# A new static order for the recorded part of a fused attention and MLP kernel: maxima apart from multiplies on Pool, transposes by TensorE, divisions on VectorE

## The chip, the cores and the metric

The kernel runs on one core of a Trainium2 chip. The metric is the device time of one execution in microseconds (us). TensorE does the matmuls, VectorE (DVE in the profile), ScalarE (ACT) and Pool (GpSimd) the element-wise work, and SyncE (SP) and Pool issue the DMAs. Runs are called fast or slow by their granted TensorE clock and time; only fast runs are compared here. Each kernel has one trace, of one of its runs: what a trace shows need not be the same in the others.

## The reference, cut to what matters

Favor attention (a random-feature softmax) over 8 batches of 8 heads with 576 tokens of 64 numbers, then a two-layer MLP with a GELU-like gate over the 4,608 tokens.

```python
def phi(x):                                   # q and k (times 64 ** -0.25), each token and head
    h = x @ omega.T - sum(x * x) / 2          # 64 -> 128 features
    return exp(h - max(h)) / sqrt(m)
kv  = einsum('bhsm,bhsd->bhmd', k_p, v);  z = sum(k_p, axis=2)
num = einsum('bhsm,bhmd->bhsd', q_p, kv)
den = einsum('bhsm,bhm->bhs', q_p, z) + 1e-06
x   = (num / den), heads side by side         # 4608 x 512
h   = x @ w_in                                # 512 -> 2048
out = (h / (1 + exp(-1.702 * h))) @ w_out     # 2048 -> 512
```

Sums over tokens make each batch of attention a unit; the MLP works on blocks of 512 tokens. A "pair" is two heads of one batch: batch 0 has pairs 0 to 3, batch 1 pairs 4 to 7, and so on. MLP block 0 needs batch 0; block 1 needs the last 64 tokens of batch 0 and most of batch 1, so all of pairs 4 to 7.

## The kernel before

The helpers that matter here are these. Both kernels have them at the same lines, so L390 or L509 in a profile is the same helper in both.

```python
def load_win(j):                               # L96, a quarter of w_in, issued by Pool
    nc.gpsimd.dma_start(win[j][:], ...)
def cast_k(b, c0, c1):                         # L160: DRAM to DRAM, float32 to bf16, issued by Pool
    nc.gpsimd.dma_start(sk[...], bass.AP(k.tensor, ...))
def cast_q(b, c0, c1): ...                     # L174: the same for q
def load_tr(b, n, c0, c1):                     # L179: DMA transpose of what the casts wrote
    nc.sync.dma_start_transpose(tiles[b][n][...], tiles[b]["s" + n][...])

def halves_max(p):                             # L390: first half of a row maximum, on VectorE
    ke = st[p, "ke"]
    nc.vector.tensor_tensor(out=half[:], in0=ke[:, :, 0:64], in1=ke[:, :, 64:128], op=ALU.max)
def maxima(p): ...                             # L395 reduce_max of half
def inverse(p): ...                            # L399 reciprocal
def scale_v(p, pool):                          # L406 and L412: v times the inverse maximum
    eng = nc.gpsimd if pool else nc.vector
    eng.tensor_tensor(out=vp[:, :, 0:64], in0=v, in1=emax, op=ALU.mult)
    eng.tensor_copy(out=vp[:, :, 64], in_=emax[:])

def nd_div(p, i, on_act=False): ...            # L461 ScalarE or L465 VectorE: num / den
def xt_pe(p, home): ...                        # L499: attention output of a pair transposed by TensorE
def xt_cp(p, on_act, c0=0, c1=S): ...          # and copied from PSUM into xt
def xt_dma(p):                                 # L509, L513: the same by two DMA transposes
    nc.sync.dma_start_transpose(dst[:, 0:512]..., xb[:, 0:4, :]...)
    nc.sync.dma_start_transpose(dst[:, 512:S], xb[64:128, 4, :])

def mm1(i, f, c0=0, c1=CM):                    # L545: w_in group f of block i; reads xt[0..3]
    for c in range(c0, c1):
        nc.tensor.matmul(ph, lhsT=win[f // 4][...], rhs=xt[c][:, i * TB : (i + 1) * TB], ...)
def gelu_th(i, f): ...                         # L561 tanh on ScalarE
def gelu_mul(i, f): ...                        # L569 multiply on VectorE, writes gTs[i][:, f]
def mm2_mms(i, r, part, home): ...             # L585: w_out, four groups f of token chunk r
```

All engines run a static order. For the first 80 us it is a recorded list of some 500 calls; after it a regular loop takes over. The old list around the start of block 1 reads:

```python
        load_v(2, 0, 2, nc.gpsimd)
        ...
        load_q(2, 2, 3)
        cast_q(3, 2, 3)
        cast_k(3, 0, 1)
        ...
        cast_q(3, 0, 1)
        kv_pe(7)
        xt_dma(4)
        ...
        xt_dma(5)
        ...
        cast_k(3, 1, 2)
        ...
        cast_q(3, 1, 2)
        mm2_store(0, 0)
        xt_dma(6)
        ...
        xt_dma(7)
        ...
        cast_k(3, 2, 3)
        load_bt(3, 0, 2)
        ...
        homes[1, 3] = "b0"
        mm1(1, 3)                              # the first w_in group of block 1
```

The softmax here doesn't subtract the row's maximum and nothing guards it: scores larger than these inputs give would overflow.

Of the kernel before, what the change touches and what calls it, by code (L numbers as in the profile page):

```python
# [21 lines left out]
def kernel(  # L22
# [16 lines left out]
    nc = tc.nc  # L39

    B, H, S, D = q.shape
# [658 lines left out]
    with tc.manual_schedule(engines={ET.DVE, ET.Activation}):  # L700
        load_k(0, 2, 3)
# [3 lines left out]
        make_identity(nc, ident[:])  # L705
        warm_mm(7, 512, "qp")
        tk_pe(0, "xx")
        q0_cast(True)
        load_q(0, 1, 2)
        om_cast(False)  # L710
        om_pe("b0")
        q0_cast(False)
        warm_mm(3, 128, "qp")
        tq_pe(0, "b1")
        tq_cp(0, True)
        om_cp(False)
        tk_cp(0, False)
        pk_pe(0)
        e_km(0)
        load_v(0, 0, 1, nc.gpsimd)  # L720
        tk_pe(1, "b0")
        tk_cp(1, False)
        tk_pe(2, "b1")
        load_q(0, 2, 3)
        tk_cp(2, False)
        pf_pe(0)
        e_k5(0)
        pq_pe(0)
        pk_pe(1)
        e_km(1)  # L730
        halves_max(0)
        load_q(0, 3, 4)
        pf_pe(1)
        tq_pe(1, "b1")
        pf_pe(2)
        maxima(0)
        e_k5(1)
        warm_mm(2, 512, "b0")
        pk_pe(2)
        load_k(0, 3, 4)  # L740
        load_v(0, 1, 2, nc.gpsimd)
        inverse(0)
        pr_pe(0)
        tq_cp(1, False)
        warm_mm(3, 128, "b0")
        pr_pe(1)
        load_k(1, 2, 3)
        e_qm(0)
        halves_max(1)
        maxima(1)  # L750
        tq_pe(2, "b0")
        tq_cp(2, False)
        warm_mm(3, 128, "b1")
        tk_pe(3, "b1")
        inverse(1)
        load_v(0, 2, 4, nc.gpsimd)
        load_k(1, 0, 1)
        tk_cp(3, False)
        e_k5(2)
        pq_pe(1)  # L760
        e_qr(0)
        e_km(2)
        halves_max(2)
        e_qm(1)
        tq_pe(3, "b0")
        load_q(1, 1, 2)
        load_k(1, 1, 2)
        tq_cp(3, False)
        load_win(0)
        pr_pe(2)  # L770
        pf_pe(3)
        scale_v(0, True)
        kv_pe(0)
        maxima(2)
        kv_cp(0)
        pk_pe(3)
        scale_v(1, True)
        warm_mm(1, 512, "b1")
        nd_pe(0, 1, "b1")
        e_qr(1)  # L780
        e_k5(3)
        inverse(2)
        scale_v(2, True)
        nd_pe(0, 0, "b0")
        nd_inv(0, 0)
        pr_pe(3)
        kv_pe(1)
        nd_inv(0, 1)
        nd_div(0, 0, False)
        e_km(3)  # L790
        halves_max(3)
        maxima(3)
        pq_pe(2)
        tk_pe(6, "kp")
        tk_cp(6, False)
        kv_cp(1)
        nd_pe(1, 0, "b0")
        nd_div(0, 1, True)
        inverse(3)
        xt_dma(0)  # L800
        nd_pe(1, 1, "b1")
        load_win(2)
        nd_inv(1, 1)
        e_qm(2)
        kv_pe(2)
        kv_cp(2)
        e_qr(3)
        scale_v(3, True)
        e_qr(2)
        nd_inv(1, 0)  # L810
        load_win(1)
        nd_div(1, 1, True)
        pq_pe(3)
        load_win(3)
        nd_div(1, 0, False)
        e_qm(3)
        tk_pe(4, "kp")
        tk_cp(4, False)
        tq_pe(5, "xx")
        load_q(1, 2, 3)  # L820
        tq_cp(5, False)
        nd_pe(2, 1, "b0")
        nd_pe(2, 0, "b1")
        pk_pe(4)
        nd_inv(2, 0)
        nd_inv(2, 1)
        nd_div(2, 0, False)
        nd_div(2, 1, False)
        load_k(2, 0, 1)
        load_q(1, 3, 4)  # L830
        kv_pe(3)
        kv_cp(3)
        xt_pe(1, "qp")
        xt_cp(1, False, 0, S2)
        xt_cp(1, False, S2, S)
        e_km(4)
        nd_pe(3, 0, "b1")
        nd_inv(3, 0)
        nd_pe(3, 1, "b0")
        homes[0, 0] = "xx"  # L840
        mm1(0, 0, 0, 1)
        nd_inv(3, 1)
        nd_div(3, 0, False)
        homes[0, 1] = "xx+"
        mm1(0, 1, 0, 1)
        mm1(0, 1, 1, 2)
        xt_pe(2, "kp")
        xt_cp(2, False, S2, S)
        tk_pe(5, "b1")
        xt_cp(2, False, 0, S2)  # L850
        nd_div(3, 1, True)
        xt_pe(3, "qp")
        xt_cp(3, False, 0, S2)
        mm1(0, 0, 1, 2)
        mm1(0, 0, 2, 3)
        homes[0, 3] = "b0"
        mm1(0, 3, 0, 1)
        xt_cp(3, False, S2, S)
        mm1(0, 1, 2, 3)
        mm1(0, 0, 3, 4)  # L860
        tk_cp(5, False)
        homes[0, 11] = "qp"
        mm1(0, 11)
        homes[0, 10] = "qp+"
        mm1(0, 10)
        gelu_th(0, 11)
        gelu_mul(0, 11)
        gelu_th(0, 0)
        gelu_th(0, 10)
        gelu_mul(0, 10)  # L870
        homes[0, 8] = "kp"
        mm1(0, 8)
        gelu_th(0, 8)
        mm1(0, 1, 3, 4)
        gelu_mul(0, 0)
        homes[0, 7] = "kp+"
        mm1(0, 7)
        gelu_th(0, 1)
        gelu_th(0, 7)
        homes[0, 4] = "b1"  # L880
        mm1(0, 4)
        gelu_mul(0, 8)
        homes[0, 9] = "qp+"
        mm1(0, 9)
        gelu_mul(0, 1)
        mm1(0, 3, 1, 2)
        gelu_th(0, 4)
        mm1(0, 3, 2, 3)
        gelu_th(0, 9)
        load_k(1, 3, 4)  # L890
        gelu_mul(0, 7)
        gelu_mul(0, 4)
        gelu_mul(0, 9)
        pk_pe(5)
        pf_pe(4)
        pf_pe(5)
        e_k5(4)
        homes[0, 12] = "b1"
        mm1(0, 12)
        halves_max(4)  # L900
        maxima(4)
        inverse(4)
        load_q(1, 0, 1)
        e_km(5)
        load_v(1, 2, 4, nc.gpsimd)
        homes[0, 6] = "qp+"
        mm1(0, 6)
        e_k5(5)
        homes[0, 13] = "kp+"
        mm1(0, 13)  # L910
        halves_max(5)
        load_v(1, 0, 2, nc.gpsimd)
        gelu_th(0, 12)
        gelu_mul(0, 12)
        load_wout(0)
        gelu_th(0, 6)
        gelu_th(0, 13)
        load_wout(1)
        gelu_mul(0, 13)
        homes[0, 14] = "qp"  # L920
        mm1(0, 14)
        gelu_th(0, 14)
        mm1(0, 3, 3, 4)
        gelu_th(0, 3)
        gelu_mul(0, 14)
        tk_pe(7, "xx")
        tk_cp(7, True)
        homes[0, 15] = "kp"
        mm1(0, 15)
        gelu_mul(0, 3)  # L930
        homes[0, 2] = "kp+"
        mm1(0, 2, 0, 1)
        load_wout(2)
        tq_pe(4, "b1")
        mm1(0, 2, 1, 2)
        mm1(0, 2, 2, 3)
        tq_cp(4, False)
        mm1(0, 2, 3, 4)
        gelu_th(0, 15)
        gelu_mul(0, 15)  # L940
        load_q(2, 0, 1)
        gelu_th(0, 2)
        tk_pe(8, "b0")
        tk_cp(8, True)
        homes[0, 5] = "b1"
        mm1(0, 5)
        gelu_th(0, 5)
        gelu_mul(0, 6)
        scale_v(4, True)
        pr_pe(5)  # L950
        pf_pe(7)
        pr_pe(4)
        pq_pe(4)
        e_qm(4)
        kv_pe(4)
        gelu_mul(0, 2)
        load_wout(3)
        pk_pe(6)
        pf_pe(6)
        e_k5(6)  # L960
        mm2_mms(0, 1, 0, "b0")
        e_k5(7)
        load_k(2, 2, 3)
        gelu_mul(0, 5)
        maxima(5)
        inverse(5)
        mm2_mms(0, 0, 0, "b1")
        kv_cp(4)
        e_km(6)
        tq_pe(6, "qp")  # L970
        tq_cp(6, False)
        halves_max(6)
        load_v(2, 2, 4, nc.gpsimd)
        mm2_mms(0, 1, 1, "b0")
        load_q(2, 1, 2)
        e_qr(5)
        e_qr(4)
        pq_pe(5)
        e_qm(5)
        maxima(6)  # L980
        inverse(6)
        pk_pe(7)
        scale_v(6, True)
        mm2_mms(0, 0, 1, "b1")
        mm2_mms(0, 0, 2, "b1")
        load_k(2, 1, 2)
        load_q(2, 3, 4)
        pr_pe(6)
        e_km(7)
        pq_pe(6)  # L990
        scale_v(5, False)
        halves_max(7)
        maxima(7)
        pf_pe(8)
        e_qm(6)
        kv_pe(5)
        e_k5(8)
        kv_cp(5)
        mm2_mms(0, 1, 2, "b0")
        nd2_pe(4, "qp")  # L1000
        mm2_mms(0, 1, 3, "b0")
        e_qr(6)
        nd2_pe(5, "xx")
        nd2_inv(4)
        nd2_div(4)
        load_v(2, 0, 2, nc.gpsimd)
        inverse(7)
        nd2_inv(5)
        tq_pe(8, "kp")
        nd2_div(5)  # L1010
        mm2_mms(0, 0, 3, "b1")
        tq_pe(7, "qp")
        scale_v(7, True)
        load_k(2, 3, 4)
        tq_cp(8, False)
        mm2_out(0, 1, True)
        tk_pe(10, "b0")
        kv_pe(6)
        pk_pe(8)
        tq_cp(7, False)  # L1020
        pq_pe(7)
        mm2_out(0, 0, True)
        tk_cp(10, False)
        load_q(2, 2, 3)
        cast_q(3, 2, 3)
        cast_k(3, 0, 1)
        mm2_mms(0, 2, 0, "b0")
        e_km(8)
        tk_pe(9, "b1")
        kv_cp(6)  # L1030
        nd2_pe(6, "xx")
        halves_max(8)
        tk_cp(9, False)
        mm2_mms(0, 2, 1, "b0")
        tq_pe(9, "b1")
        pk_pe(9)
        nd2_inv(6)
        nd2_div(6)
        e_qm(7)
        tq_cp(9, False)  # L1040
        pq_pe(8)
        pr_pe(7)
        e_km(9)
        cast_q(3, 0, 1)
        kv_pe(7)
        xt_dma(4)
        pf_pe(9)
# [276 lines left out]
```

## Time and profile before

| | before |
|---|---|
| time, median of three runs | 320.04 us (319.91 to 320.26) |
| profiled span | 317.0 us, clock 1.0 |
| TensorE busy | 309.5 us, 98% |
| VectorE, ScalarE, Pool busy | 197.4, 189.0, 86.1 us |
| longest maximum by halves | 2.14 us (median 459 ns) |

The stretches below show busy time of each engine with its instructions, granted clock, DMA share (over 1 where queues overlap in the records), and GB/s.

```profile
18.00:24.00 6.00, 5.41 (x86) 4.05 (x86) 5.08 (x20) 4.37 (x14) 5.72 (x9) 1.00 1.22 163
...
54.00:60.00 6.00, 6.00 (x79) 3.48 (x78) 5.00 (x12) 4.71 (x12) 0.18 (x1) 1.00 1.31 219
60.00:66.00 6.00, 6.00 (x72) 3.34 (x69) 3.56 (x7) 5.59 (x10) 3.36 (x6) 1.00 1.21 182
66.00:72.00 6.00, 6.00 (x98) 3.59 (x98) 5.62 (x14) 5.78 (x13) 1.32 (x2) 1.00 1.16 292
```

The timeline of TensorE (start, duration, engine, line, operation and tiles, count, and in brackets idle time with what ended it) at the start of block 1 and at the seam with the loop has no bracket at all:

```profile
61.86 0.38 PE L284 MATMUL pq<-qT,omT 64*128 64x512 bf16 x2
62.18 1.04 PE L545 MATMUL ph<-xt,win 128*128 128x512 bf16 x4
63.06 0.47 PE L441 MATMUL nd<-kvs,qe 128*128 128x65 bf16 x10
...
80.45 1.03 PE L585 MATMUL po<-wout,gT 128*128 128x512 bf16 x4
```

The change aims at the maxima. The view of one tile gives minimum, median and maximum in ns, and Pool's timeline shows what ran at the time of the long one (11.82 to 13.96 us):

```profile
L390 DVE TENSOR_TENSOR half<-ke x32: 397/459/2143, 8.0 to 231.0; 128x576 bf16<-128x576 bf16 x32
```

```profile
11.24 1.17 POOL L406 TENSOR_TENSOR vp<-vst,emax 128x576 bf16<-128x576 f32 x1
...
12.50 1.14 POOL L406 TENSOR_TENSOR vp<-vst,emax 128x576 bf16<-128x576 f32 x1
```

### The profile page before, as it was taken

Reading aid. Unit: us, or ns where it says so; the run is one execution under the profiler, and the core shown is the slowest. Engines: PE = TensorE matmul, PEld = TensorE weight load, DVE = VectorE, ACT = ScalarE, POOL = GpSimd, SP = SyncE. Lnnn points to the kernel's source line nnn. Section 1 sums busy time; section 2 is a strip of 40 time slices with the busy share of each in tenths; the row PEclk is TensorE's granted clock in tenths of the full one; section 3 lists DMA queues with packets and bytes.
Section 4 is the critical chain, followed back from the end, with each engine's and each line's share of the span. In section 5 each row is a group of like instructions: output and inputs, shape, how many; then the busy total and the mean of one; then the engine's idle time right before and its main releaser. Section 6 shows DMA issues by size and latency. Waiting matters only on the chain.

```text
span 317.0 us, 6672 instructions
## 1 busy us (share of the span) xinstructions
PE 309.5 (98%) x2647; PEld 165.2 (52%) x2647; DVE 197.4 (62%) x379; ACT 189.0 (60%) x364; POOL 86.1 (27%) x154
## 2 busy tenths in 40 slices
PE   8889999999999999999999999999999999999995
PEld 4565556555455555555555455555555444444444
DVE  3987878699566666666666666677774343343400
ACT  4887866897566666666666666666653434444311
POOL 8795446413511161116110430001010100001100
PEclk9999999999999999999999999999999999999999
DMA  8999999998798679775979395911122100001121
GB/s 189 249 170 221 272 244 223 204 261 143 98 297 170 133 199 209 141 126 156 227 102 190 74 274 135 193 54 35 54 35 64 57 35 33 34 33 35 47 85 67
DMA packets 61742, 44.13 MB, mean 139 GB/s; under 512 B 46161, under 2 KB 54736, under 8 KB 61392
## 3 DMA queue, kind: packets, MB, share of 16 engines
q0 software_dynamic: 13552, 24.55, 37.1%
q1 hardware_dynamic: 47888, 19.10, 29.0%
q8 instruction: 20, 0.33, 0.4%
q10 hardware_dynamic: 272, 0.07, 0.1%
q14 instruction: 10, 0.08, 0.1%
HBM read 37.42 MB, written 15.66 MB: 167 GB/s over the span
## 4 chain that ended last, share of the span: by engine, by line
PE 93%; DVE 3%; DMA 2%; ACT 0%; issue 0%; ACTq 0%; DVEq 0%
PE ph L545 40%; PE po L585 38%; PE xx L226 3%; PE nd L441 3%; PE pk L269 3%; PE pq L284 2%; DMA xt<-xb 2%; PE po L622 1%; PE warm_ps L681 1%; DVE half L390 1%; PE tk L198 1%; PE tq L211 1%; DVE maxE L395 1%; DVE qT L191 0%; DVE kT L191 0%; PE xx L284 0%
## 5 line engine op out<-in xcount | busy, mean ns | idle before, releaser
L545 PE MATMUL ph<-xt,win 128*128 128x512 bf16 x576 | 145.2, 379 | 0.2 <-DMA xt<-xb 0.2
L561 ACT ACTIVATE th<-ph 128x512 bf16<-128x512 f32 x144 | 86.2, 608 | 92.8 <-PE ph L545 92.7
L585 PE MATMUL po<-wout,gT 128*128 128x512 bf16 x560 | 141.5, 379 | 0.0
L569 DVE SCALAR_TENSOR_TENSOR gT<-th,ph 128x512 bf16<-128x512 bf16 x144 | 97.0, 684 | 63.3 <-ACT th L561 63.1
L545 PEld LDWEIGHTS <-win 128*128 128x128 bf16 x576 | 62.8, 114 | 55.1 <-DMA xt<-xb 0.7
L585 PEld LDWEIGHTS <-gT 128*128 128x128 bf16 x560 | 52.4, 98 | 59.0 <-issue 0.3
L608 POOL DMA_DIRECT2D out_dram<-osb x44 | 23.6, 539 | 178.2 <-ACT osb L598 175.2
L360 ACT ACTIVATE ke<-pk 128x1024 bf16<-128x1024 f32 x32 | 32.9, 1028 | 2.1 <-PE pk L269 2.0
L372 ACT ACTIVATE qe<-pq 128x1024 bf16<-128x1024 f32 x32 | 33.1, 1035 | 1.6 <-PE pq L284 1.5
L390 DVE TENSOR_TENSOR half<-ke 128x576 bf16<-128x576 bf16 x32 | 16.8, 524 | 26.8 <-ACT ke L369 23.6
L598 ACT ACTIVATE osb<-po 128x512 f32<-128x512 f32 x35 | 21.0, 599 | 18.7 <-PE po L585 18.6
L395 DVE TENSOR_REDUCE maxE<-half 128x9 f32<-128x576 bf16 x32 | 24.1, 753 | 0.9
L484 DVE TENSOR_TENSOR xb<-nd,rden 128x640 bf16<-128x640 f32 x28 | 23.1, 824 | 0.9
L406 POOL TENSOR_TENSOR vp<-vst,emax 128x576 bf16<-128x576 f32 x12 | 14.2, 1179 | 27.8 <-DVE emax L399 16.3
L441 PEld LDWEIGHTS <-qe 128*128 128x128 bf16 x320 | 14.0, 98 | 8.1 <-issue 1.5
L441 PE MATMUL nd<-kvs,qe 128*128 128x65 bf16 x320 | 15.6, 194 | 1.3 <-ACT xb L461 0.6
L226 PE MATMUL xx<-vp,ke 64*128 64x65 bf16 x576 | 15.8, 191 | 0.5 <-POOL vp L412 0.4
L406 DVE TENSOR_TENSOR vp<-vst,emax 128x576 bf16<-128x576 f32 x20 | 15.1, 757 | 0.8
L226 PEld LDWEIGHTS <-ke 64*128 64x128 bf16 x576 | 13.1, 95 | 2.1 <-issue 1.3
L269 PEld LDWEIGHTS <-qk 64*128 64x128 bf16 x180 | 7.6, 119 | 9.5 <-issue 6.9
L160 POOL DMA_DIRECT2D sk<-in_k_dram x20 | 10.9, 544 | 0.0
L174 POOL DMA_DIRECT2D sq<-in_q_dram x20 | 10.4, 518 | 0.0
(60 smaller groups left out, 183.9 us busy)
## 6 DMA issues: line engine op xcount, KB each, us to landing
vst<-in_v_dram SPq DMA_DIRECT2D x5, 1152.0 KB, 8.9
out_dram<-osb POOLq DMA_DIRECT2D x12, 256.0 KB, 2.4
sk<-in_k_dram POOLq DMA_DIRECT2D x19, 160.0 KB, 7.5
vst<-in_v_dram POOLq DMA_DIRECT2D x5, 576.0 KB, 8.9
sq<-in_q_dram POOLq DMA_DIRECT2D x20, 144.0 KB, 7.7
win<-in_moe_w_in_dram POOLq DMA_DIRECT2D x4, 512.0 KB, 7.5
wout<-in_moe_w_out_dram POOLq DMA_DIRECT2D x4, 512.0 KB, 10.1
out_dram<-osb POOLq DMA_DIRECT2D x10, 192.0 KB, 2.9
```

What stands on the lines that cost most here:

```text
L226: yield lambda t=t: nc.tensor.matmul(kv[:, i, :], lhsT=ke[lo : lo + 64, t, :], rhs=vp[lo : lo + 64, t, :], start=(t == 0), stop=(t == KT - 1),
L360: nc.scalar.activation(out=ke_tile(p)[:, 0:8, :].rearrange("p (c s) f -> p s c f", s=2), in_=st.pop((p, "pk"))[:].rearrange("p s (c f) -> ...
L372: nc.scalar.activation(out=qe_tile(p)[:, :, :, 0:256], in_=st.pop((p, "pq"))[:].rearrange("p s (i r) -> p s i r", i=2), func=AF.Exp, scale ...
L395: nc.vector.reduce_max(out=maxE[:], in_=st.pop((p, "half"))[:], axis=AX.X)
L406: eng.tensor_tensor(out=vp[:, :, 0:64], in0=tiles[b]["v"][:, c, :].rearrange("p (t d) -> p t d", d=D), in1=emax[:].unsqueeze(2).to_broadca ...
L441: nc.tensor.matmul(nd[:, t, :], lhsT=st[p, "qe"][:, i, c0 : c0 + 128], rhs=st[p, "kvs"][:, i, :])
L484: nc.vector.tensor_tensor(out=xb_tile(p)[:].rearrange("p t (i d) -> p i t d", i=2), in0=nd[:, :, :, 0:64], in1=st.pop((p, "rden2"))[:].uns ...
L545: mm = nc.tensor.matmul(ph, lhsT=win[f // 4][:, c, f % 4 : 512 : 4], rhs=xt[c][:, i * TB : (i + 1) * TB], start=(c == 0), stop=(c == CM - 1),)
L561: act = nc.scalar.activation(out=th[:], in_=ph_tile(i, f), func=AF.Tanh, scale=0.851)
L569: dve = nc.vector.scalar_tensor_tensor(out=gTs[i][:, f, :], in0=th[:], scalar=1.0, in1=ph_tile(i, f), op0=ALU.add, op1=ALU.mult)
L585: nc.tensor.matmul(pos[i, r][:], lhsT=gTs[i][:, f, r * 128 : (r + 1) * 128], rhs=wout[:, f, :], start=(f == 0), stop=(f == NFC - 1),)
L608: eng.dma_start(out[row : row + (n - 1) * step + 1 : step, :], osb[p0 : p0 + n, :])
```

## The change

The new list keeps every helper and the whole loop. It is meant to keep the maxima by halves and Pool's multiplies of v apart in time, to bring the outputs of batch 0 back by TensorE's transposes only (pair 0 went by DMA), and to put all divisions of batch 0 on VectorE. As everything is one list, about 540 lines move. The core of the diff, with cuts; lines are in the order of the list:

```diff
-        warm_mm(7, 512, "qp")
+        warm_mm(5, 512, "qp")
 ...
+        halves_max(0)                 # ahead of Pool's first multiply
 ...
-        nd_div(0, 1, True)
+        nd_div(0, 1, False)           # division on VectorE
-        xt_dma(0)
+        xt_pe(0, "qp")
+        scale_v(3, True)              # on Pool
+        nd_inv(1, 1)
+        nd_div(1, 1, False)
+        load_win(2)                   # Pool issues these two behind its multiplies
 ...
+        xt_cp(0, True, 0, S2)
+        load_win(1)
 ...
+        load_v(2, 2, 4, nc.gpsimd)    # batch 2's last load of v, now here
 ...
+        xt_dma(5)
+        cast_q(3, 1, 2)               # seven casts of batch 3, not six
+        cast_q(3, 0, 1)
 ...
+        cast_k(3, 1, 2)
+        xt_dma(4)
 ...
+        cast_k(3, 0, 1)
+        cast_k(3, 2, 3)
+        xt_dma(6)
+        xt_dma(7)
+        cast_k(3, 3, 4)
+        cast_q(3, 3, 4)
+        load_bt(3, 0, 2)
 ...
-        homes[1, 14] = "qp"           # the list ended with group 14 of block 1
-        mm1(1, 14)
-        gelu_mul(1, 14)
+        homes[1, 2] = "kp"            # it now ends with group 2
+        mm1(1, 2)
+        gelu_th(1, 2)
+        gelu_mul(1, 11)
+        gelu_mul(1, 6)
+        gelu_mul(1, 2)
```

## The prediction

> **What bounds it now.** The page has TensorE busy 309.5 of 317.0 us and the chain that ended last 93% TensorE, but a matmul's record (379 ns at 512 columns) is longer than its spacing (216 ns). Counting matmuls at their steady spacing, I get 290.7 us of useful TensorE work; some 26 us are idle, dummies or drain. Before 22 us only 8.5 us are useful (13.5 lost); from 22 to 80 us about 4.5 are lost; later 0.3 per 10 us (bound by TensorE, code unchanged). So only the recorded order of the first 80 us can move.
>
> There VectorE and ScalarE are full: from 10 to 20 us they are busy 9.65 and 8.93 us. The chain of waits holds a halves-maximum of 2.06 us (at 11.91), a ScalarE division (15.45), a DMA transpose of 4.93 us (16.35), then dense matmuls from 22.9.
>
> **What the change does.**
> - Halves-maximum: median 459 ns, but two take 2.14 and 1.06 us, at 11.82 and 15.74, while Pool multiplies v (11.24 to 13.64, 15.32 to 16.47). The Trainium skill, "SBUF — State Buffer", section "Who interferes with whom", says a VectorE instruction with two SBUF inputs contends with a Pool instruction that reads SBUF; the trace agrees. At most 2.3 us of VectorE are saved; the new order may still let the third and fourth overlap.
> - Three divisions leave ScalarE (1.14 us each) for VectorE (0.49): ScalarE gains 3 us, VectorE pays 1.4.
> - The DMA transpose of pair 0 becomes five TensorE transposes (0.28 us) and two ScalarE copies (about 0.5 us), so w_in matmuls wait for less.
> - Fewer warm-up matmuls at the head: five of 512 columns, not seven.
> - Pieces of pairs 4 and 5 move forward.
>
> Walking the new order by hand with these durations, the last quarter of batch 0 is copied at about 22 us, not 23.6, with nine w_in matmuls done instead of three: 2.4 us ahead at best. The walk has no stalls, so I count 1.6. From 22 to 80 us I grant 0.5 more (a contended 1.14 us VectorE copy at 43.25 goes).
>
> **What it gives back.** At the seam with the loop (80 us) the order now ends with w_in group 2 of block 1, and the loop's first w_out matmuls need groups 0 to 3. TensorE's third weight load waits for VectorE: after the last w_in matmul come tanh 0.60 and multiply 0.69, where weights are due in 0.65 us. Before, nothing waited here. Estimate: 1.1 us lost.
>
> Net: 1.2 us less. **318.8 us, 8 times in 10 within 316.8 to 320.8.** Faster by over 2% 0.03, within 2% 0.95, slower 0.02.
>
> **Shown right or wrong by.**
> 1. Halves-maximum mean falls from 524 to below 485 ns, its longest from 2.14 to below 1.1 us.
> 2. Dense TensorE work from 20 to 21 us instead of 22.9.
> 3. No DMA transpose before 40 us.
> 4. A TensorE idle of about 1 us at the loop's first w_out, released by VectorE.
> 5. From there to the end the same length within 0.3 us.
>
> **What would make it wrong.** The clock: before, the spacing of 128 columns falls from 107 to 56 ns at 6.6 us. The skill, "TensorE: Matmul & The Clock Gate", Part 1, asks about 3.4 us of sustained activity; with a shorter head and a gap after it, early steps may stay at double time for longer. Or the second w_in quarter, issued near 18 us and landing 7 to 8 us later, is late for group 11 near 25 us. Or the middle has bubbles that I didn't walk.

## More of the kernel before

The page of the kernel before gives busy time and share of the span for each engine, then a map of the span in 40 slices of 7.9 us (DMA is the mean busy share of 16 engines, in tenths), then the chain of work that ended last, by engine and by line.

```profile
PE 309.5 (98%) x2647; PEld 165.2 (52%) x2647; DVE 197.4 (62%) x379; ACT 189.0 (60%) x364; POOL 86.1 (27%) x154
...
DMA  8999999998798679775979395911122100001121
...
PE 93%; DVE 3%; DMA 2%; ACT 0%; issue 0%; ACTq 0%; DVEq 0%
```

The chain says TensorE. But read the DMA row with it: its first ten slices stand at 8 or 9, to 79 us. The 16 DMA engines are as full in the recorded part as TensorE. The chain gives DMA only 2%, because nothing waits for what lands just in time.

Group 3 of block 1 starts at 62.18 us. Its fourth matmul, which starts at 62.85, waits for the first transpose of pair 7, and that lands, by the DMA records, at 62.72 us. There is 0.13 us of slack. (The second transpose of each pair has the last 64 tokens of the batch, which block 2 reads; that of pair 7 lands at 62.94.)

## The result, and the profile after

| | before | after |
|---|---|---|
| median | 319.98 us (319.27 to 320.26, 4 runs) | 327.19 us (4 runs; fast ones 327.05, 327.18, 327.21; one slow, 334.45) |
| profiled span, clock | 317.0 us, 1.0 | 325.4 us, 1.0 |
| TensorE busy | 309.5 us, 98% | 309.9 us, 95% |
| VectorE, ScalarE busy | 197.4, 189.0 us | 198.7, 188.7 us |

The ratio is 1.0228, with a 95% interval of 1.0207 to 1.0248: the new order is slower by over 2%. (A ratio here is the mean time of one kernel's fast runs over that of the other's fast runs of the same rounds, so not quite the ratio of the medians.) The result is correct, and the same work is done: the busy times of TensorE, VectorE and ScalarE agree within 1.3 us, and Pool's fell from 86.1 to 83.0.

The page of the kernel after, same lines as before:

```profile
PE 309.9 (95%) x2656; PEld 165.6 (51%) x2656; DVE 198.7 (61%) x382; ACT 188.7 (58%) x355; POOL 83.0 (25%) x150
...
DMA  8999999997992659894977597821214010001031
...
PE 73%; DMA 17%; DVE 6%; ACT 2%; issue 1%; POOL 0%; ACTq 0%
PE po L585 34%; PE ph L545 29%; DMA xt<-xb 7%; DMA wout<-in_moe_w_out_dram 4%; PE pk L269 2%; PE nd L441 2%; PE xx L226 2%; DMA qk<-sk 2%; DMA win<-in_moe_w_in_dram 2%; DVE gT L569 1%; PE pq L284 1%; PE po L622 1%; DVE half L390 1%; DVE xb L484 1%; DMA om_f<-in_omega_dram 1%; DVE maxE L395 1%
```

DMA's part of the chain rises from 2% to 17%, and the largest part of it, 7%, is the transposes `xt<-xb`. TensorE's timeline shows five waits after 60 us, where the kernel before had none:

```profile
63.46 0.62 PE L545 MATMUL ph<-xt,win 128*128 128x512 bf16 x2 [1.47 <-DMA xt<-xb]
64.72 0.80 PE L545 MATMUL ph<-xt,win 128*128 128x512 bf16 x2 [0.64 <-DMA xt<-xb]
...
69.89 0.25 PE L269 MATMUL xx<-omT,qk 64*128 64x128 bf16 x1 [2.04 <-DMA qk<-sk]
...
86.30 1.21 PE L585 MATMUL po<-wout,gT 128*128 128x512 bf16 x4 [1.02 <-DVE gT L569]
...
90.28 0.38 PE L545 MATMUL ph<-xt,win 128*128 128x512 bf16 x1 [2.12 <-DMA xt<-xb]
```

The brackets start at the modelled end of a matmul. Measured from start to start, less the steady spacing of the matmul ahead (216 ns for 512 columns), the five gaps are 1.63, 0.81, 2.20, 1.19 and 2.29 us, 8.1 together. All gaps below are given in this way. They are nearly the whole of the 8.4 us by which the span grew, as a count of useful TensorE work shows (each matmul at its steady spacing, dummies left out):

```
useful TensorE us done by   22 us   60 us   72 us   80 us   95 us
before                       8.50   44.30   55.36   62.92   77.81
after                        8.92   44.49   51.18   58.57   69.89
```

At 22 us the new order is 0.42 us ahead, at 60 us 0.19, and at 95 us it is 7.9 behind. The early gain was 0.4, not 1.6, because the maxima are not apart after all:

```profile
L390 DVE TENSOR_TENSOR half<-ke x32: 396/458/1695, 7.9 to 239.4; 128x576 bf16<-128x576 bf16 x32
```

```profile
12.82 1.16 POOL L406 TENSOR_TENSOR vp<-vst,emax 128x576 bf16<-128x576 f32 x1
...
15.67 1.16 POOL L406 TENSOR_TENSOR vp<-vst,emax 128x576 bf16<-128x576 f32 x1 [0.66 <-DVE emax L399]
```

Two maxima, at 12.62 and 16.00 us, still fall together with Pool's multiplies and take 1.70 and 1.13 us. A 1.54 us gap on TensorE at 15.53 us follows, released by a copy of VectorE that came late.

The stretches of the kernel after, to be laid beside those of before:

```profile
18.00:24.00 6.00, 5.43 (x103) 3.77 (x99) 5.57 (x20) 3.92 (x11) 5.38 (x9) 1.00 0.87 135
...
54.00:60.00 6.00, 6.00 (x76) 3.19 (x76) 3.19 (x7) 4.71 (x9) 1.32 (x2) 1.00 0.93 148
60.00:66.00 6.00, 3.85 (x54) 2.20 (x51) 2.87 (x8) 3.27 (x6) 1.77 (x3) 1.00 1.12 154
66.00:72.00 6.00, 3.96 (x60) 2.37 (x59) 4.45 (x10) 2.87 (x6) 0.00 (x0) 1.00 1.17 177
```

DMA is busy 0.87 in 18 to 24 us, against 1.22, and moves 148 GB/s in 54 to 60 us, against 219. The DMA queue of SyncE holds all transposes. Its issues in the kernel before:

```profile
47.33 1.21 SPq L509 DMA_TRANSPOSE xt<-xb  x1
...
50.12 1.26 SPq L509 DMA_TRANSPOSE xt<-xb  x1
...
56.50 1.22 SPq L509 DMA_TRANSPOSE xt<-xb  x1
57.76 1.81 SPq L513 DMA_TRANSPOSE xt<-xb  x1
59.90 1.63 SPq L179 DMA_TRANSPOSE qk<-sk  x1
```

And in the kernel after:

```profile
46.29 1.32 SPq L509 DMA_TRANSPOSE xt<-xb  x1
...
49.67 1.31 SPq L509 DMA_TRANSPOSE xt<-xb  x1
...
54.37 1.22 SPq L509 DMA_TRANSPOSE xt<-xb  x1
55.63 1.55 SPq L513 DMA_TRANSPOSE xt<-xb  x1
58.23 1.74 SPq L509 DMA_TRANSPOSE xt<-xb  x1
60.31 1.46 SPq L513 DMA_TRANSPOSE xt<-xb  x1
63.49 1.18 SPq L179 DMA_TRANSPOSE qk<-sk  x1
```

By the DMA records, the transpose issued at 46.29 us lands at 58.16, 11.9 us later, and the first of pair 4, issued at 49.67, at 63.41 (13.7 us). Before, the first of pair 4 took 5.4 us and the first of pair 5 7.5. Each late issue stands just behind a landing: 58.23 behind the one at 58.16, 60.31 behind 60.29, 63.49 behind 63.41. The waits of that queue name the semaphores of DMAs that it issued eight DMAs earlier. So one late transpose also holds back the issue of later ones: batch 3's transpose (`qk<-sk`) goes out at 63.49 and not 59.90, lands at 69.85 and not 63.78, and is the 69.89 wait.

What delays the first ones shows in the packets. Batch 2's last load of v is in flight to 55.35 us (before: 52.16), then seven casts, issued from 48.59 to 52.51 us, land up to 63.49. Counted in the trace, packets that start in Pool's queue (loads and casts, mostly 1,280 bytes in this stretch) and in SyncE's (transposes, 256 bytes, with some stores of 2,048 bytes among them: most of the 49 of before at 57 to 58 us):

```
packets per us in   55-56    57-58    61-62    62-63    63-64
after   Pool           61      139       20        1        0
after   SyncE          48      142      324      412      655
before  Pool           99       83        0        0        0
before  SyncE          38       49      808      927     1113
```

While both queues have work, about as many packets start in one as in the other; when Pool's runs dry, the transposes run many times as fast. The Trainium skill, "DMA: Bandwidth & Descriptors", section "Queues, rings and completion order", says that each DMA engine goes round the queues it has work for, a packet at a time. The counts fit that: 139 to 142 from 57 to 58 us. So a transpose of many small packets, issued beside a burst of casts with larger ones, lands when the casts are done.

These turns may not be the whole delay. Between 52.0 and 56.1 us of the kernel after, eleven packets of 9,216 bytes (of the casts of q) took 2.9 to 3.9 us each, where all 48 of the kernel before took 0.70. From 53 to 54 us only 26 packets of both queues started, and from 52 to 56 us the DMA engines moved 127 GB/s, against 225. Such long packets (8 to 13 of them over 2 us) stand in just those fast traces below whose first transpose takes over 10 us (e2, e4, e7); e1 and f1 have three and one, and f2 ten of v's load. What holds them no run shows.

### The profile page after: what moved, and what is told of

It reads as the page before. It is cut to its first block, busy times and chain, and to the rows that moved or that the text cites. A ratio compares the mean times of both kernels' runs of the same rounds, so it can differ in the third digit from the quotient of the medians.

```text
span 325.4 us, 6662 instructions
## 1 busy us (share of the span) xinstructions
PE 309.9 (95%) x2656; PEld 165.6 (51%) x2656; DVE 198.7 (61%) x382; ACT 188.7 (58%) x355; POOL 83.0 (25%) x150
## 4 chain that ended last, share of the span: by engine, by line
PE 73%; DMA 17%; DVE 6%; ACT 2%; issue 1%; POOL 0%; ACTq 0%
PE po L585 34%; PE ph L545 29%; DMA xt<-xb 7%; DMA wout<-in_moe_w_out_dram 4%; PE pk L269 2%; PE nd L441 2%; PE xx L226 2%; DMA qk<-sk 2%; DMA win<-in_moe_w_in_dram 2%; DVE gT L569 1%; PE pq L284 1%; PE po L622 1%; DVE half L390 1%; DVE xb L484 1%; DMA om_f<-in_omega_dram 1%; DVE maxE L395 1%
## 5 line engine op out<-in xcount | busy, mean ns | idle before, releaser
L598 ACT ACTIVATE osb<-po 128x512 f32<-128x512 f32 x33 | 19.8, 599 | 16.5 <-PE po L585 16.5
L406 POOL TENSOR_TENSOR vp<-vst,emax 128x576 bf16<-128x576 f32 x10 | 11.6, 1160 | 31.9 <-DVE rden L480 17.3
L406 DVE TENSOR_TENSOR vp<-vst,emax 128x576 bf16<-128x576 f32 x22 | 16.7, 758 | 1.0 <-DMA vst<-in_v_dram 0.3
L243 ACT ACTIVATE kvs<-xx 128x130 bf16<-128x130 f32 x32 | 9.5, 298 | 2.3 <-PE xx L226 2.3
```

The source lines that it names most:

```text
L406: eng.tensor_tensor(out=vp[:, :, 0:64], in0=tiles[b]["v"][:, c, :].rearrange("p (t d) -> p t d", d=D), in1=emax[:].unsqueeze(2).to_broadca ...
```

## The experiments

The theory after reading the two traces: the loss lies in the later part of the new list (from the end of block 0's w_in), where the order of DMA issues lets block 1's transposed inputs land late; the seam adds a microsecond. The rivals: the gain and loss of the first part (maxima, w_in loads), TensorE's own new order, and late loads of v. The texts give the theory and its rivals a letter each and say what it stands for. Every kernel below gave a correct result. The old kernel ran beside each: the medians of the jobs were 319.95 (e1 to e4), 320.49 (e5 to e7 and c1), 320.33 (e8, c2 to c4) and 318.92 us (f1 to f3 and c5), so kernels of different jobs are compared by their ratios. All fast runs of e1, e2, e5 and e7 had a granted clock of 0.986 to 0.995, so their times may be somewhat high; in e5 they rise from 324.92 us at 0.994 to 328.66 at 0.986.

### The two parts apart: e1_head_after and e2_head_before

The list is cut where block 0's last w_in group has been multiplied. e1 has the new first part and the old rest, e2 the old first part and the new rest.

```diff
 e1: after.py with the rest of the list from before.py
 e2: before.py with the rest of the list from after.py
```

> The new order up to the end of block 0's w_in work (about 38 us), then the old order for the rest. Theory T (the loss is made in the second half of the order: block 1's DMA transposes land behind batch 2's loads and batch 3's casts): no TensorE wait for a DMA transpose of 1 us or more after 60 us, 318.5 to 321 us. Rival R (the new head issues its second and fourth w_in quarters 3 us later and leaves DMA idle at 18 to 24 us, and everything later is late by that): the waits near 62 and 68 us stay, 324 to 328 us.

> The old order up to the end of block 0's w_in work, then the new order. T: the TensorE waits for xt and qk transposes between 60 and 91 us appear (4 us or more in sum), 325 to 328 us. R: they are gone, 319 to 321 us.

e1 took 325.29 us (325.15 to 325.85), ratio 1.0179 (1.0147 to 1.0211). That was a miss for the theory's number, and the profile tells why it is no clean test: the new first part loads batch 2's first k later than the old rest uses it.

```profile
42.49 0.45 PE L198 MATMUL tk<-ident,qk 128*128 128x128 bf16 x5 [2.38 <-DMA qk<-in_k_dram]
```

Its gap is 2.65 us, with two behind it 4.25 together; after 60 us there is none. e2 took 326.27 us (fast runs 325.27 to 327.18), ratio 1.0194 (1.0147 to 1.0240):

```profile
64.28 0.60 PE L545 MATMUL ph<-xt,win 128*128 128x512 bf16 x2 [1.39 <-DMA xt<-xb]
...
66.02 1.01 PE L545 MATMUL ph<-xt,win 128*128 128x512 bf16 x2 [1.14 <-DMA xt<-xb]
```

Its gaps of 1.55, 1.31, 1.19 (seam) and 2.03 us (at 90.50) stand where the new kernel's do, but for the one at 70 us, which is missing. Time and waits are as the theory has it. So the new rest makes these waits with the old first part too, and the first part is not their sole cause.

### Block 1's inputs without DMA: e3_xt_by_pe

```diff
-        xt_dma(5)
+        xt_pe(5, "b1")
+        xt_cp(5, False)
 ...
+        xt_pe(4, "b0")
+        xt_cp(4, False)
 ...
-        xt_dma(4)
 (pairs 6 and 7 in the same way)
```

> The changed kernel with the four DMA transposes of pairs 4 to 7 done by TensorE and VectorE, nothing else moved. T: the wait of 2.1 us at 62 us goes, the batch 3 transposes issue earlier so the wait at 68 us shrinks below 1 us, and that at 90 us shrinks too; TensorE pays 1.1 us: 321 to 324 us. R: only the xt waits go, the data of batch 3 stay late: 325 us or more.

324.64 us (323.37 to 325.25), ratio 1.0148 (1.0110 to 1.0186), between the two ranges that were foretold. No wait on a DMA is left after 60 us, and batch 3's transpose is issued at 58.22, not 63.49. But the added transposes wait for PSUM banks that others hold (gaps of 0.82, 0.46 and 0.66 us at 51.89, 55.83 and 60.26), and the seam's 1.19 stays. The waits on DMA are real; this remedy pays for itself only in part.

### The maxima really apart: e4_apart

Two maxima run into Pool's multiplies, because the reciprocals that release Pool come early. Moved back, they start Pool after the maximum.

```diff
         e_qr(0)
-        inverse(1)
 ...
         halves_max(2)
+        inverse(1)
 ...
         halves_max(3)
+        inverse(2)
```

> The changed kernel with two VectorE reciprocals moved behind the third and fourth halves-maximum, so that Pool's multiply cannot start before these have run. Both halves-maxima should take below 0.6 us (1.70 and 1.13 now). T: TensorE is 0.5 to 1.5 us ahead at 30 us, but it then waits that much longer for the transposes at 62 us: within 0.7 us of the changed kernel. Rival (the port conflict in the head counts in full): 1.2 to 1.9 us faster than the changed kernel.

The tile's view shows that this does what the change intended:

```profile
L390 DVE TENSOR_TENSOR half<-ke x32: 398/458/577, 7.7 to 235.4; 128x576 bf16<-128x576 bf16 x32
```

Useful TensorE work at 22 us is then 10.66 us (after: 8.92). It took 325.38 us (323.22 to 326.42), ratio 1.0167 (1.0111 to 1.0223). That is 1.8 us below the changed kernel of the first job, which is the rival's number, and 0.4% by ratio below the changed kernel run again (f3, 1.0208), with intervals that overlap; so the time decides neither way. In its trace, of its fastest run, TensorE waits 2.41 us at 62.27 for the same transposes, then 0.72 and 0.43: in front of block 1 it waits 1.1 us longer than before this edit, as the theory has it. But the waits at 70 and 90 us are not in this trace, which the theory did not foretell.

### The casts later: e5_casts_late

```diff
         xt_dma(5)
-        cast_q(3, 1, 2)
-        cast_q(3, 0, 1)
 ...
+        cast_k(3, 0, 1)               # all seven behind xt_dma(7)
+        cast_q(3, 0, 1)
+        cast_k(3, 1, 2)
 ...
```

> The changed kernel with batch 3's seven casts issued by Pool after the multiply of pair 9 (about 57 us) and not after that of pair 7 (48 us), so block 1's DMA transposes have no casts beside them. T (transposes share the DMA engines with the casts and land when these are done): the transposes of pairs 5 and 4, which now land 11.9 and 13.7 us after issue, land within 9 us; the wait at 63 us falls from 2.4 to below 0.8 us; batch 3's data come later, so the wait near 69 us grows from 2.2 to 3 us or more; in sum 325.5 to 328.5 us. If the casts are innocent, the landings stay above 11 us.

326.66 us (324.92 to 328.66), ratio 1.0184 (1.0134 to 1.0235). The transposes of pairs 5 and 4 take 7.9 and 5.1 us, not 11.9 and 13.7, and the wait at 63 us is gone; the data of batch 3 are late in return (a gap of 4.02 us at 68.58, on `qk<-sk`). These and the time are as the theory foretold: the casts hold up the transposes, and moving the casts only moves the wait.

### v earlier: e6_v_early

```diff
-        load_q(2, 2, 3)
+        load_v(2, 0, 2, nc.gpsimd)
 ...
-        load_q(2, 0, 1)
+        load_v(2, 2, 4, nc.gpsimd)
 (batch 2's three q loads take the later places)
```

> The changed kernel with the same seven loads of batch 2 by Pool between 40 and 47 us in another order: v first and third, not last, as the old kernel has them spread. Theory V (v's 9 KB packets, in flight together with the transposes' 256-byte packets, hold most DMA engines for 3 us at 52 us): no such hole, the casts end 1.5 us earlier or more, the wait at 63 us is below 1 us: 324 to 326 us. T by volume alone: the same volume is ahead of the transposes, so within 0.7 us of the changed kernel.

Fast runs of 323.57, 323.90 and 327.17 us, ratio 1.0127 (1.0065 to 1.0188). The wait at 64 us stays (2.00 us), the one at 70 us is gone in the profiled run, and the one near 90 us is 1.26. The packets of 9 KB that theory V puts down to v belong to the casts of q; those of v's load are of 4,608 bytes. None takes over 2 us here, so the hole is gone, but the casts end only 0.8 us earlier and the wait is not below 1 us: V is missed, and the time (one run within 0.7 us of the changed kernel, as the other forecast has it, two some 3 us below) settles nothing. With this spread the run does not say how much v's place is worth; it does say that v's late load alone is not what makes the first wait.

### The seam: e7_seam

```diff
-        homes[1, 14] = "qp"
-        mm1(1, 14)
+        homes[1, 2] = "qp"            # group 2 earlier, group 14 last
+        mm1(1, 2)
 ...
-        homes[1, 2] = "kp"
-        mm1(1, 2)
+        homes[1, 14] = "kp"
+        mm1(1, 14)
```

> The changed kernel with w_in groups 2 and 14 of block 1 exchanged in the order, so that the loop's first w_out matmuls do not wait for the last gelu. The wait of 1.2 us at 86 us falls below 0.5. T: the next w_in group then waits longer for the DMA transpose that lands at 90.2 us (2.3 us now, 3 us then): within 0.5 us of the changed kernel. Rival (the waits add up): 0.8 us or more faster.

325.62 us (324.85 to 327.60), ratio 1.0158 (1.0109 to 1.0208), but the seam's gap stayed at 1.19 us (at 87.76). The last group but one, group 6, is needed second by the loop, and it holds the bank that the loop's first output takes. The swap was too small to remove the wait, so this run says nothing about its worth. (The wait at 90 us is not in its trace; whether by the swap or by chance no run tells.)

### The w_in loads earlier: e8_win_early

In 18 to 24 us the DMA engines of the new kernel are underused: Pool issues the last two w_in quarters at 19.84 and 21.30 us, behind two multiplies that wait for VectorE.

```diff
+        load_win(2)
         scale_v(2, True)
 ...
+        load_q(1, 0, 1)
+        load_win(1)
         scale_v(3, True)
 ...
-        load_win(2)
-        load_q(1, 0, 1)
 ...
-        load_win(1)
```

> The changed kernel with the second w_in quarter, a q and the fourth quarter issued by Pool before the multiplies of pairs 2 and 3 that they stood behind, so that the DMA engines are not underused from 18 to 24 us. R (lost DMA time early makes everything late): the landings near 46 us and the waits at 63 to 91 us move by 2 us, 324 to 325.5 us. T: DMA is full from 24 us on in either kernel and the two kernels are level at 46 us, so the waits near 63, 69 and 90 us stay 4 us or more in sum, 326 to 328 us.

Fast runs of 324.29, 324.86 and 324.91 us, ratio 1.0145 (1.0116 to 1.0175). The quarters go out at 15.35 and 18.32 us, 5.22 MB have moved by 24 us (after: 4.78), and the last transpose of pairs 4 to 7 lands at 63.17 us, not 65.31; the wait at 63 us is gone, the one on `qk<-sk` remains (2.06 us at 67.62), and so does the one near 90 us (2.44 at 88.16). The result is divided: the time is in R's range, and the waits that remain are 4.5 us in sum, as T has it. So earlier loads at 15 to 18 us do take away the wait at 63 us. That the idle DMA engines make a part of the loss is not shown by that: up to 24 us the kernel before had moved hardly more than the one after (203 against 199 GB/s on average, and 218 in e8), and e2, with the old first part, has the waits all the same.

### Only the casts moved in the old kernel: f1_casts_in_before and f2_casts_v_in_before

All runs so far repair the new kernel. These two put the suspected cause into the old one and leave TensorE's order untouched.

```diff
 f1 (before.py):
+        cast_k(3, 1, 2)
+        cast_q(3, 1, 2)
+        cast_k(3, 2, 3)
+        cast_q(3, 3, 4)
         xt_dma(4)
 (and taken out at their old places)
 f2 (f1, and):
-        load_v(2, 0, 2, nc.gpsimd)
 ...
         load_q(2, 2, 3)
+        load_v(2, 0, 2, nc.gpsimd)
         cast_q(3, 2, 3)
```

> The kernel before, with only four of batch 3's casts pulled ahead of the first transposes of block 1 (seven issued by about 49 us, as the new order does, instead of spread to 60 us). TensorE's order is untouched. Theory U (casts in the queues hold up block 1's transposes): transposes of pairs 4 and 5 take 8 us or more from issue to landing instead of 5.2 to 7.5, a wait of 1 to 2.5 us on a DMA transpose opens on TensorE between 60 and 66 us, and the time is 321.5 to 324 us. Rival R (the waits come of how the new order arranges TensorE's own work): no new wait over 0.5 us, 319.5 to 320.8 us.

> As f1_casts_in_before, and batch 2's last load of v is put behind the last load of q, directly ahead of the casts, as in the new order. U: the transposes land later still, the wait at 60 to 66 us grows by 0.5 to 1.5 us over f1, 322 to 325 us. R: 319.5 to 320.8 us.

f1 took 320.91 us (319.25 to 321.57) where the old kernel's median was 318.92, ratio 1.0046 (1.0004 to 1.0087). One wait appears:

```profile
62.26 0.38 PE L284 MATMUL pq<-qT,omT 64*128 64x512 bf16 x2
64.61 1.02 PE L545 MATMUL ph<-xt,win 128*128 128x512 bf16 x4 [1.97 <-DMA xt<-xb]
```

Its gap is 2.24 us (TensorE gets there 0.4 us later than in the kernel before), in the place and of the kind that the theory foretold; the first transpose of pair 5 takes 8.8 us, not 7.5, while those of pair 4 stay near 5 (I had expected 8 for them too). By the issue times, all that differs is one cast more in the burst, seven instead of six. The time lies between the two ranges, 0.1 us above the rival's and 0.6 under the theory's (and the old kernel of that job 1 us under that of the others), so the verdict rests on the wait in one trace, which the rival has no room for. It shows the mechanism without any change of TensorE's order, at a size of 0.46%, against 2.28% for the new order.

f2 took 325.41 us (323.67 to 326.31), ratio 1.0176 (1.0129 to 1.0223), and its wait is of another kind than I expected:

```profile
60.51 0.67 PE L226 MATMUL xx<-vp,ke 64*128 64x65 bf16 x18 [3.82 <-DVE vp L412]
```

The late v itself, landing at 59.50 us, holds up the multiply of pair 8 and with it TensorE (a gap of 3.98 us). So it is a miss as a dose test, and its clock was lower in three of four runs (0.989).

Laid side by side, the runs show when the transposes of pairs 4 to 7 are done (block 1 waits for the last but one, which lands 0.2 us earlier in before and after; c1 and c2 come further below; e1's last landing is not in its trace):

```
                    casts in   last of them   last transpose of      gap on TensorE
                    burst      landed, us     pairs 4-7 landed, us   near 63 us for xt
c2_combined            6         59.18           61.98               none
before                 6         61.45           62.94               none
e8_win_early           7         61.86           63.17               none
c1_combined            6         61.81           63.59               none
e4_apart               7         61.97           64.02               2.41 + 0.72
e6_v_early             7         62.66           64.52               2.00
after                  7         63.49           65.31               1.63 + 0.81
f1_casts_in_before     7         63.88           65.36               2.24
e7_seam                7         63.52           65.38               1.72 + 0.60
e2_head_before         7         65.29           66.54               1.55 + 1.31
f2_casts_v_in_before   7         67.02           68.26               none (3.98 for v)
e5 (casts behind)      7         66.49           63.57               none
```

Where the casts go out ahead of or among the transposes, the last transpose lands 1.2 to 2.8 us after the last cast, whatever else was changed; in e5, where the casts go out behind them, the order is the other way about.

### The changed kernel again: f3_after_again

> The changed kernel again, unaltered, for its spread and for whether its waits stand at the same places: 327.0 to 327.4 us in the fast state, waits on DMA transposes at 63 to 65 (2.4 us together), 70 (2.2) and 90 us (2.3), and 1.2 us at the seam.

Fast runs of 325.38, 325.39 and 326.72 us, ratio 1.0208 (1.0163 to 1.0253), and one slow run of 334.12, which took the profile; its waits are therefore not used. The loss repeats; the time was 0.3 to 1.8 us below that of the first job, so under the range foretold, and the old kernel's was 1.1 us lower too.

### The new order with its causes removed: c4_new_mended and c5_new_mended_seam

c4 is the new list with e4's and e7's edits and with pairs 4 to 7 transposed by TensorE in banks that are free at the time. c5 also mends the seam in earnest.

```diff
 c4 (after.py with e4 and e7):
         tq_cp(9, False)
+        xt_pe(5, "b0")
+        xt_cp(5, False)
 ...                                   (pairs 4, 6, 7 likewise, no xt_dma)
 c5 (c4, and):
-        homes[1, 12] = "xx"
-        mm1(1, 12)
         homes[1, 6] = "b0"
         mm1(1, 6)
 ...
+        homes[1, 12] = "xx"
+        mm1(1, 12)
```

> The changed kernel with the three causes mended and its order otherwise kept: reciprocals behind the halves-maxima (e4), block 1's transposes by TensorE in banks that are free (e3, better placed), groups 2 and 14 exchanged at the seam (e7). T: no wait of 1 us after 30 us apart from a rest at the seam; 319 to 321.5 us. If the loss has another cause, it stays above 322.5 us.

> c4_new_mended with the seam mended properly: the last two w_in groups are 12 and 14, which the loop needs last, and the bank that the loop's first output takes is not one of theirs. If the seam wait is the last of the four causes, it goes (c4 had 1.20 us at 83.7), nothing else changes, and the time is 319.6 to 320.2 us, that is the old kernel's within 0.2%. If 320.8 us or more, a cause is still missing.

c4 took 321.06 us (320.64 to 321.99), ratio 1.0036 (1.0008 to 1.0064). Of the 2.28% that the new order lost, 1.9 are back. Its one gap over 0.5 us after 20 us is the seam, 1.20. It differs from e4 (1.0167) by the transposes and by e7's swap, which left the seam's gap as it was, and their intervals do not meet: so with the maxima apart, taking these transposes off the DMA queues is worth 1.3%. c5 took 320.97 us beside an old kernel of 318.92, ratio 1.0053 (1.0023 to 1.0084): no gain over c4, and against the line drawn beforehand. The seam's gap shrank to 0.77 us, but a wait on w_out opened at 39.19 us (1.57 us; 0.46 in c4). So what the seam is worth was not shown, and the last 0.4% is open.

### The good parts alone: c1_combined, c2_combined and c3_two_by_pe

c1 takes the new first part with e4's edit, issues batch 2's first k and the w_out quarters in time for the old rest, and keeps the old rest. c2 mends three small waits that c1's profile showed; c3 also takes two pairs off the DMA queues.

```diff
 c1 (new first part, old rest):
+        load_k(2, 0, 1)
-        load_wout(2)
+        load_wout(1)
 c2 (c1, and):
-        pq_pe(5)
+        mm2_mms(0, 0, 0, "b1")
         mm2_mms(0, 1, 0, "b0")
         inverse(5)
+        scale_v(5, True)
 ...
+        pq_pe(5)
         e_qm(5)
 c3 (c2, and):
-        xt_dma(6)
+        xt_pe(6, "b1")
+        xt_cp(6, False)
 (pair 7 likewise)
```

> A version meant to beat both: the new head with the port conflict taken out (as in e4), batch 2's first k loaded before the second w_out quarter (its lateness made the 2.65 us wait of e1 at 42.5 us), then the old order. T: TensorE is about 1.5 us ahead at 38 us, no wait above 1 us after it: 317.5 to 320 us. If the DMA engines' volume alone sets the time when block 1's inputs land, it waits near 60 us and gives it back: 319.5 to 322 us.

> The combined version with three small waits near 38 to 46 us taken out (a projection later, two w_out groups in the other order, one multiply on Pool). T: TensorE reaches block 1's first w_in matmul 1.5 us earlier and waits there for the last DMA transposes that land at 63 to 63.6 us: gain 0 to 1 us over the combined version, 318.5 to 319.8 us.

> As the one before, and pairs 6 and 7, the last two DMA transposes that block 1 waits for, done by TensorE and VectorE (0.6 us of TensorE). T: no wait for xt at 60 to 64 us and batch 3's transposes issue earlier: 317.5 to 319.3 us.

c1 took 319.76 us (319.30 to 320.58), ratio 0.9970 (0.9943 to 0.9997), where both of its forecasts overlap; it does not wait near 60 us. c2 took 318.50 us (317.94 to 318.89, six runs), ratio 0.9953 (0.9931 to 0.9974), and so beats both kernels, the old one by 0.5%. Its chain and its start of block 1:

```profile
PE 92%; ACT 3%; DMA 2%; DVE 1%; issue 1%; ACTq 0%
```

```profile
61.21 1.02 PE L545 MATMUL ph<-xt,win 128*128 128x512 bf16 x4
62.07 0.47 PE L441 MATMUL nd<-kvs,qe 128*128 128x65 bf16 x10
```

The transpose that the fourth matmul waits for lands at 61.37 us, the last one at 61.98, and group 3 starts at 61.21 without a wait. c3 took 320.31 us, ratio 1.0012 (0.9990 to 1.0034), a miss: a wait of 1.09 us on Pool's multiply opened at 62.63.

## Why the prediction was wrong

**The step that failed is "From 22 to 80 us I grant 0.5 more".** I granted a gain of 0.5 us to a stretch that I had not walked; by 80 us it had lost 4.8 us against its state at 22 us (4.35 behind instead of 0.42 ahead, from the count of useful work), and its late DMA issues another 2.3 at 90 us. The step rested on "There VectorE and ScalarE are full", which left the DMA engines out, although their row in the map was full. With DMA share at 1.2 to 1.3 in 48 to 66 us and a last input that lands at 62.72 for a matmul that starts at 62.85, the order of DMA issues was as much on the critical path as TensorE's. The prediction named "the middle has bubbles that I didn't walk" as what would make it wrong; it gave a loss of over 2% a probability of 0.02.

**"I count 1.6" for the first part** was mis-sized: 0.42 us at 22 us. The halves were not kept apart in the new list (1.70 and 1.13 us remain). I wrote that the third and fourth "may still" overlap and did not look. e4, where they are apart, has 1.7 us more useful work at 22 us than the new kernel, so the size was right for an order that does what this one intends. What that gain is worth in the end e4 leaves open: its transposes were still late at 62 us.

**"Estimate: 1.1 us lost" at the seam** was right: 1.19 us of gap, 1.02 by the timeline, released by VectorE.

Point by point:

1. Mean of the maxima below 485 ns, longest below 1.1 us: wrong. 518 ns and 1.70 us. The rule used, the Trainium skill, "SBUF — State Buffer", section "Who interferes with whom", agrees with the trace: 577 ns at most in e4, where they are kept apart, and 1.06 to 2.14 us beside a multiply of Pool's.
2. Dense work from 20 to 21 us: wrong by about 1.5 us. The first w_in matmul of block 0 starts at 20.55 (before: 21.42), but the first long run of them at 22.56 (before: 22.90).
3. No DMA transpose before 40 us: right, the first is at 46.29.
4. An idle of about 1 us at the seam, released by VectorE: right.
5. From the seam to the end the same length within 0.3 us: wrong. From the loop's first w_out matmul, 80.45 to 317.0 is 236.6 us before, and 86.30 to 325.4 is 239.1 after. The difference is the 2.3 us wait on `xt<-xb` at 90.28, for which the DMA queues of the list are still answerable: that transpose was issued at 83.80, not 77.58, beside a burst of casts that starts at 83.0.

The risks named: the clock may have played a small part. The Trainium skill, "TensorE: Matmul & The Clock Gate", Part 1, asks for about 3.4 us of sustained activity; TensorE reached its short spacing at about 8.0 us and not 6.6 (6.6 and 5.1 us after its first dummy matmul at 1.46, longer than the page's figure in both), which agrees with a head that has fewer dummies; no run tests it. The w_in quarters were not late for their own matmuls (the last landed at 29.23 us), but issued earlier (e8) they took away the wait at 63 us.

What is shown: the casts in the queues delay block 1's transposes (f1, e5, and the table), this makes the waits at 63 to 65 us (e2, e5, f1), and without these DMA transposes most of the loss is back (c4 against e4). That earlier w_in loads take away the first wait is one run (e8); that the early idle of the DMA engines makes a part of the loss is not shown. That the delayed queue of SyncE carries the delay on to the wait at 70 us is read from the issue and landing times; e3, which takes eight transposes out of it, agrees (58.22, no wait), but was not made for this alone. How the loss divides among these causes is not settled: removals of one cause gave ratios from 1.0127 to 1.0184, with intervals that overlap, and the waits move. 0.4% of the new order remains unexplained after c4 and c5.

## What to carry to other kernels

Before moving instructions in a tuned static order, write down for each stage when the last input lands and when it is used; where that slack is near zero and the DMA map is full, a DMA issue is on the critical path even if the chain of waits gives DMA 2%. Keep bursts of large transfers behind small-packet transposes that are needed soon (e5 shows the price: what the burst brings comes later in turn), and walk the whole part that the change touches, not only the part that it is meant to improve. Test a suspected order from both sides: repairs of the slow kernel moved the waits about, and four casts moved in the fast kernel opened the wait.

## What the Trainium skill lacked or had wrong

- "DMA: Bandwidth & Descriptors", section "Queues, rings and completion order", has the turn-taking by packets, and the counts fit it. It lacks the consequence for a DMA transpose beside plain DMAs: the trace's records for one are of 256 bytes, and beside records of 1,280 bytes a transpose of pairs 4 and 5 took 11.9 to 13.7 us instead of 5.2 to 7.5. Records of both queues started in about equal number (139 to 142 in one us), whereas the page has a packet of about 9 to 17 descriptors; whether a record here is such a packet, and whether they took turns one by one, no run shows.
- "DMA: Bandwidth & Descriptors", section "Rules for kernel authors", says that a DMA transpose next to ordinary DMAs needs nothing; it speaks there of silently wrong results. The results were correct in all runs, so that holds for correctness; for time it cost 2.4 us of waits at 63 to 65 us.
- No page that I read has the limit that SyncE's queue showed: it issued a DMA only when the one eight earlier had landed (58.23 us behind 58.16, 60.31 behind 60.29, 63.49 behind 63.41). In the trace this is a wait of the program itself, on one of eight semaphores that the queue's DMAs take in turn (for the issues at 58.23 and 63.49 a wait instruction of its own at 58.18 and 63.43 us). So it is not shown to be a limit of the chip, and may be nothing that the skill lacks.
- "SBUF — State Buffer", section "Who interferes with whom", was right, but gives no time for this pair of instructions. Here the maximum by halves took 0.46 us alone and 1.06 to 2.14 us beside a Pool multiply of 1.15 us.
